# Three fused stages on one core: the RMS norm's group sum, mean and reciprocal root go from TensorE, ScalarE and VectorE to GpSimd

## The chip, the core and the metric

One core of a Trainium2 chip. A core has five engines with a queue each, in order: TensorE (PE), VectorE (DVE), ScalarE (ACT), GpSimd (POOL) and SyncE (SP, which only issues DMAs here). PE reads SBUF and writes PSUM, of which eight banks of 128 x 512 float32 are used: four (mm) for products on the way, four (acc) for sums. The metric is the time of one execution in device microseconds; lower is better.

## What is computed

```python
def _attn_ref(q, k, v, tau):            # N = 6016 rows, C = 256
    qn = q / (np.linalg.norm(q, axis=1, keepdims=True) + 1e-06)
    kn = k / (np.linalg.norm(k, axis=1, keepdims=True) + 1e-06)
    s = kn.transpose(0, 2, 1) @ qn / tau
    ...
    return (v @ a).astype(np.float32)   # a: softmax of s over the last axis

def _moe_ref(x, w_in, w_out):           # 256 -> 2048 -> 256
    h = np.maximum(x @ w_in, 0.0)
    return (h * h @ w_out).astype(np.float32)

def _moe2_ref(x, w_gate, w_val, w_out, rms_g):   # 256 -> 1536 -> 256
    rms = np.sqrt(np.mean(x * x, axis=-1, keepdims=True) + 1e-06)
    xn = x / rms * rms_g
    g = xn @ w_gate
    silu = g * (1.0 / (1.0 + np.exp(-g)))
    val = xn @ w_val
    return (silu * val @ w_out).astype(np.float32)
```

The output is `_moe2_ref(_moe_ref(_attn_ref(...)))`. The change touches `rms` and `xn` alone. Products are made in float32 quality from parts: each operand is split into a high and a low part, and three products (high by high, high by low, low by high) are added.

## The kernel before

The activations lie transposed: channels on the partitions (256 channels are two tiles of 128), rows of x along the free axis. The 6016 rows are twelve blocks (ten of 512, two of 448) in six pairs. The program runs through: the attention matrix (to some 55 us); the first MLP, blocks 0 to 3 one by one in units of `mlp1`, in which one hidden tile takes six matmuls up and six down; the first MLP for pairs 2 to 5 in `mlp1_pair`, which multiplies a pair as 2 x 2 blocks with seven products in place of eight, eight groups to a pair; the second MLP in `mlp2`, with the same seven products, twelve groups to a pair, most pairs in two visits.

Nothing is scheduled by a planner: the code writes out the order of every engine's queue. Work beside the products is a list of steps, `side` (norms and the operands made from the normed x) and `tokens` (the next pair's v operands, or weights). A group of `mlp1_pair` calls `aside()` at three places, after its second, its fifth and its last product, and each call takes one step from either list. In the second MLP a group has four such places, shared with `flow`, a list of weight preparation with lags.

A norm exists for each of blocks 0 to 3 (`norm_steps`) and each of pairs 2 to 5 (`pair_norm`). Its steps: s1 squares both channel tiles (ACT); s2 adds them and transposes 32 x 32 blocks (DVE); s3 sums runs of 32 on DVE, which leaves on partition 32i + t the sum over 32 channels of row t of a group, four such partial sums (i = 0 to 3) to a row, in `ns` (128 x 16, or 128 x 32 for a pair); s4 multiplies `ns` with `mean_w` on PE, which adds the four, divides by 256 and writes the mean to all four groups of partitions, after which ACT takes the root and DVE the reciprocal; s5 transposes the result back, spread over 32 (DVE); s6 multiplies x by it and by g (DVE, two instructions for a block, four for a pair).

s4 needs a bank of PSUM. In the units of `mlp1` it takes the next one in turn. In a group of the pairs it gets `b0` at a fixed place, and the step after it is taken at once:

```python
            if side and getattr(side[0], "takes_bank", False):
                side.pop(0)(b0)()
            aside()
```

`aside` takes no step from `side` as long as the first one there is an s4. ACT's root needs another table of functions than the Silu of the second MLP, so the last pair's norm loads that one again (`silu_table`). The step order of a pair is s1, s1, s2, s2b, s3, s4, s5, s6 four times, and then `pair_steps`, which make the seven operands of the normed pair, split them and store them to DRAM. L1417 and L881 are the DVE instructions that make the low part of a squared hidden tile, which the matmuls down (L110 to L112) read; L1473 and L1494 add on DVE from a bank; L1660 and L1649 are the like in the second MLP.

Of the kernel before, what the change touches and what calls it, by code (L numbers as in the profile page):

```python
# [28 lines left out]
def attn_moe_kernel(ctx: ExitStack, tc, q, k, v, tau, w_in, w_out, w_gate, w_val, w2, rms_g, out):  # L29
# [59 lines left out]
    for i in range(4):  # L89
        nc.gpsimd.tensor_tensor(out=mean_w[:, i], in0=ident[:, 0:32], in1=ident[:, 32:64], op=ALU.add)  # L90
        for j in (2, 3):
            nc.gpsimd.tensor_tensor(
                out=mean_w[:, i], in0=mean_w[:, i], in1=ident[:, 32 * j : 32 * j + 32], op=ALU.add
            )
    mw = mean_w.rearrange("p i e -> p (i e)")
    nc.gpsimd.tensor_scalar(out=mw, in0=mw, scalar1=1.0 / C, scalar2=1.0, op0=ALU.mult, op1=ALU.mult)
# [819 lines left out]

    def pair_state(p):
        if p not in xst:
            xst[p] = xp.tile([P, NC7, NB], F32, tag="xst", name="xst")
        return xst[p]  # L920

    def norm_steps(b, y):
# [26 lines left out]
        def s3():  # L949
            nc.vector.tensor_reduce(  # L950
                out=st["sm"][0], in_=st["w"][1].rearrange("p (g t) -> p g t", t=32), axis=AX.X, op=ALU.add
            )

        def s4(bank=None):
            ms = (mm() if bank is None else bank)[:, :G]
            nc.tensor.matmul(ms, mw, st["sm"][0], start=True, stop=True)

            def root():
                x, r = st["sm"]
                nc.scalar.activation(out=x, in_=ms, func=AF.Sqrt, bias=eps)  # L960
                nc.vector.reciprocal(out=r, in_=x)

            return root

        s4.takes_bank = True
# [15 lines left out]
    def pair_norm(p):  # L981
# [35 lines left out]
        def s3():  # L1017
            nc.vector.tensor_reduce(out=st["sm"][0], in_=turned(st["q"]), axis=AX.X, op=ALU.add)

        def s4(bank):  # L1020
            ms = bank[:, :G]
            nc.tensor.matmul(ms, mw, st["sm"][0], start=True, stop=True)

            def root():
                x, r = st["sm"]
                nc.scalar.activation(out=x, in_=ms, func=AF.Sqrt, bias=eps)
                if last:
                    silu_table()
                nc.vector.reciprocal(out=r, in_=x)

            return root

        s4.takes_bank = True
# [13 lines left out]
        for f in (s2, s2b, s3, s5):  # L1047
            f.only = "dve"
        return [only("act", s1(0)), only("act", s1(1)), s2, s2b, s3, s4, s5] + [
# [1105 lines left out]
```

## Time and profile before

| | |
|---|---|
| median of 3 runs | 1105.18 us (1105.12 to 1105.35) |
| the profiled execution | 1105.12 us, span of its instructions 1103.3 us |
| granted clock of PE over the span | 0.998 |
| busy: PE, DVE, ACT, POOL | 1093.5, 828.5, 788.3, 38.8 us |
| instructions on PE | 5122 matmuls with a weight load each |

The span runs from the first to the last instruction; the time of an execution also has what lies around it. Matmuls overlap in the records (each is listed with about 0.39 us, and the next starts 0.23 us later), so PE's progress is read from the distance of starts.

### The profile page before, as it was taken

What the parts mean: (1) busy time and instruction counts of PE and PEld (TensorE: products, weight loads), DVE (VectorE), ACT (ScalarE), POOL (GpSimd) and SP (SyncE); (2) the same over time, 40 slices, a digit from 0 to 9 for tenths busy, and PEclk for the clock granted to TensorE, in tenths of its full rate; (3) what the DMA queues carried; (4) which work ended last, traced back from release to release, by engine and by line L of the source; (5) the groups of instructions that cost most, each with busy time, mean ns of one, the idle gap of its engine ahead of it and who ended that gap; (6) DMA issues with size and microseconds to landing.
All of it is one profiled execution on the core that took longest, in us unless ns stands there. A gap on an engine that the chain in (4) does not pass through costs nothing.

```text
span 1103.3 us, 14660 instructions
## 1 busy us (share of the span) xinstructions
PE 1093.5 (99%) x5122; PEld 922.8 (84%) x5122; DVE 828.5 (75%) x1305; ACT 788.3 (71%) x1441; POOL 38.8 (4%) x72
## 2 busy tenths in 40 slices
PE   9999999999999999999999999999999999999997
PEld 8978888888788888889988888888888888888997
DVE  7988888778968968979858878686556666565655
ACT  8788888787777877877868777676655555655554
POOL 2021101000000000000000000000000000000000
PEclk9999999999999999999999999999999999999999
DMA  9643222231461471460385665204323232404001
GB/s 349 214 115 97 77 58 86 68 105 58 161 222 40 160 244 42 156 237 20 124 300 220 220 226 194 72 26 168 125 67 133 77 133 60 144 23 121 20 20 34
DMA packets 115819, 138.33 MB, mean 125 GB/s; under 512 B 52001, under 2 KB 73505, under 8 KB 115617
## 3 DMA queue, kind: packets, MB, share of 16 engines
q1 hardware_dynamic: 113472, 136.54, 36.8%
q10 hardware_dynamic: 2272, 0.85, 0.3%
q8 instruction: 40, 0.66, 0.2%
q14 instruction: 35, 0.28, 0.1%
HBM read 91.10 MB, written 46.27 MB: 125 GB/s over the span
## 4 chain that ended last, share of the span: by engine, by line
PE 95%; DVE 3%; ACT 1%; DMA 0%; issue 0%; DVEq 0%; ACTq 0%
PE mm L1555 31%; PE acc L111 13%; PE acc L112 13%; PE acc L110 13%; PE mm L1427 12%; PE mm L112 3%; PE mm L110 2%; PE mm L111 2%; PE mm L662 1%; PE acc L671 1%; PE acc L670 1%; PE acc L672 1%; PE mm L795 1%; DVE sh L1417 0%; DMA qraw<-in_k_dram 0%; DVE p L1414 0%
## 5 line engine op out<-in xcount | busy, mean ns | idle before, releaser
L1555 PE MATMUL mm<-p,gv 128*128 128x512 f32 (+1 forms) x1188 | 301.9, 387 | 0.0
L1555 PEld LDWEIGHTS mm<-p,gv 128*128 128x128 f32 x1188 | 221.9, 188 | 44.8 <-DVE hp L1635 1.0
L1660 DVE TENSOR_TENSOR sh<-hp,sh 128x512 fp32r<-128x512 f32 (+1 forms) x144 | 98.9, 687 | 111.2 <-ACT sh L1656 110.2
L1610 ACT COPY mm<-mm 128x512 f32<-128x512 f32 (+1 forms) x72 | 40.4, 562 | 157.6 <-PE mm L1555 153.6
L111 PE MATMUL acc<-sh,wo_h 128*128 128x512 f32 (+1 forms) x384 | 148.4, 386 | 0.4 <-DVE sh L1417 0.4
L110 PE MATMUL acc<-sh,wo_h 128*128 128x512 f32 (+1 forms) x384 | 148.3, 386 | 0.0
L112 PE MATMUL acc<-sh,wo_l 128*128 128x512 f32 (+1 forms) x384 | 148.2, 386 | 0.0
L110 PE MATMUL acc<-sh,w_h 128*128 128x512 f32 (+1 forms) x284 | 109.5, 385 | 0.0
L111 PE MATMUL acc<-sh,w_h 128*128 128x512 f32 (+1 forms) x284 | 109.5, 385 | 0.0
L112 PE MATMUL acc<-sh,w_l 128*128 128x512 f32 (+1 forms) x284 | 109.4, 385 | 0.0
L1417 DVE TENSOR_TENSOR sh<-p,sh 128x512 fp32r<-128x512 f32 (+1 forms) x127 | 85.8, 676 | 19.8 <-ACT p L1412 7.9
L1656 ACT CAST sh<-hp 128x512 fp32r<-128x512 f32 (+1 forms) x144 | 89.0, 618 | 2.8 <-DVE hp L1644 1.9
L1408 ACT ACTIVATE sh<-p 128x512 fp32r<-128x512 f32 (+1 forms) x127 | 78.6, 619 | 11.6 <-DVE p L1473 9.1
L111 PEld LDWEIGHTS acc<-sh,wo_h 128*128 128x128 f32 x384 | 72.1, 188 | 14.9 <-DVE sh L1417 0.8
L112 PEld LDWEIGHTS acc<-sh,wo_l 128*128 128x128 f32 x384 | 72.1, 188 | 13.7 <-DVE wo_l L182 0.3
L110 PEld LDWEIGHTS acc<-sh,wo_h 128*128 128x128 f32 x384 | 72.1, 188 | 13.4
L1555 PE MATMUL mm<-xs,gv 128*128 128x512 f32 (+1 forms) x324 | 82.6, 381 | 0.0
L1414 DVE TENSOR_TENSOR p<-p 128x512 f32<-128x512 f32 (+1 forms) x79 | 53.3, 675 | 31.8 <-ACT p L1465 31.6
L1644 DVE TENSOR_TENSOR hp<-mm,sg 128x512 f32<-128x512 f32 (+1 forms) x72 | 48.9, 679 | 34.1 <-PE mm L1555 33.4
L1635 DVE TENSOR_TENSOR hp<-mm,pu 128x512 f32<-128x512 f32 (+1 forms) x72 | 49.0, 680 | 28.0 <-ACT pu L1634 27.9
L1555 PEld LDWEIGHTS mm<-xs,gv 128*128 128x128 f32 x324 | 60.8, 188 | 10.2
L881 DVE TENSOR_TENSOR sh<-p,sh 128x512 fp32r<-128x512 f32 x64 | 45.7, 714 | 28.0 <-ACT sh L874 25.8
(282 smaller groups left out, 2178.0 us busy)
## 6 DMA issues: line engine op xcount, KB each, us to landing
p<-xd SPq DMA_DIRECT2D x102, 256.0 KB, 4.4
xd<-xp SPq DMA_DIRECT2D x66, 256.0 KB, 2.2
xs<-xd SPq DMA_DIRECT2D x12, 512.0 KB, 5.6
out_dram<-ot SPq DMA_DIRECT2D x40, 128.0 KB, 2.3
qraw<-in_q_dram SPq DMA_DIRECT2D x13, 384.0 KB, 7.2
qraw<-in_k_dram SPq DMA_DIRECT2D x13, 384.0 KB, 7.6
raw<-in_moe_w_out_dram SPq DMA_DIRECT2D x9, 512.0 KB, 3.6
raw<-in_moe_w_in_dram SPq DMA_DIRECT2D x8, 512.0 KB, 3.7
```

The lines of the kernel that those rows point to most:

```text
L110: nc.tensor.matmul(o, wh, xh, start=start, stop=False)
L111: nc.tensor.matmul(o, wh, xl, start=False, stop=False)
L112: nc.tensor.matmul(o, wl, xh, start=False, stop=stop)
L1408: nc.scalar.activation(out=st["h"], in_=r, func=AF.Square)
L1414: nc.vector.tensor_tensor(out=q, in0=r, in1=r, op=ALU.mult)
L1417: nc.vector.tensor_tensor(out=st["l"], in0=q, in1=f32(st["h"]), op=ALU.subtract)
L1427: nc.tensor.matmul(bank, m_part(a, w, g), x, start=start and j == 0, stop=j == 2, skip_group_check=not start)
L1555: nc.tensor.matmul(bank, c[:, hl, a, fs], x, start=start and j == 0, stop=j == 2, skip_group_check=not start)
L1635: add(out=h22, in0=bh, in1=w, op=ALU.add)
L1644: dve(out=h21, in0=bv, in1=sg1, op=ALU.mult)
L1656: nc.scalar.copy(out=parts[t][0], in_=x)
L1660: dve(out=pl, in0=x, in1=f32(ph), op=ALU.subtract)
```

## The change

The matrix `mean_w` goes; its tile now holds the constant -0.5 in its first part and room for copies in its second. Behind s3, a new function `invert` issues eight operations on POOL: copy partitions 64 to 127 down and add them, copy 32 to 63 down and add them, scale by 1/256 and add 1e-6, raise to the power -0.5, and copy the result of 32 partitions to the next 32 and then of 64 to the next 64. s4 remains as a step that issues nothing (two such steps for the last pair), so s5 follows one place later than s3's successor. It no longer asks for a bank, so it is taken at any place. The root on ACT, the reciprocal on DVE and the last pair's second load of the Silu table are gone.

```diff
@@ -86,14 +86,7 @@
     nc.gpsimd.memset(ones, 1.0)
 
     mean_w = wp.tile([P, 4, 32], F32, name="mean_w")
-    for i in range(4):
-        nc.gpsimd.tensor_tensor(out=mean_w[:, i], in0=ident[:, 0:32], in1=ident[:, 32:64], op=ALU.add)
-        for j in (2, 3):
-            nc.gpsimd.tensor_tensor(
-                out=mean_w[:, i], in0=mean_w[:, i], in1=ident[:, 32 * j : 32 * j + 32], op=ALU.add
-            )
-    mw = mean_w.rearrange("p i e -> p (i e)")
-    nc.gpsimd.tensor_scalar(out=mw, in0=mw, scalar1=1.0 / C, scalar2=1.0, op0=ALU.mult, op1=ALU.mult)
+    nc.gpsimd.memset(mean_w[:, 0], -0.5)
 
     eps, g_sb, tau_sb, rden = few[:, 0:1], few[:, 16 : 16 + KC], few[:, 32:33], few[:, 48 : 48 + KC]
     nc.gpsimd.memset(eps, 1e-6)
@@ -914,6 +907,19 @@
             nc.gpsimd.memset(x, 0.0)
         return [x[:, i, :G] for i in range(2)]
 
+    def invert(sm):
+
+        x, r = sm
+        G = x.shape[1]
+        minus_half, y, a = mean_w[:32, 0, :G], mean_w[:, 1, :G], x[:32]
+        for n in (64, 32):
+            nc.gpsimd.tensor_copy(out=y[:n], in_=x[n : 2 * n])
+            nc.gpsimd.tensor_tensor(out=x[:n], in0=x[:n], in1=y[:n], op=ALU.add)
+        nc.gpsimd.tensor_scalar(out=a, in0=a, scalar1=1.0 / C, scalar2=1e-6, op0=ALU.mult, op1=ALU.add)
+        nc.gpsimd.tensor_tensor(out=r[:32], in0=a, in1=minus_half, op=ALU.pow)
+        for n in (32, 64):
+            nc.gpsimd.tensor_copy(out=r[n : 2 * n], in_=r[:n])
+
     def pair_state(p):
         if p not in xst:
             xst[p] = xp.tile([P, NC7, NB], F32, tag="xst", name="xst")
@@ -950,19 +956,10 @@
             nc.vector.tensor_reduce(
                 out=st["sm"][0], in_=st["w"][1].rearrange("p (g t) -> p g t", t=32), axis=AX.X, op=ALU.add
             )
-
-        def s4(bank=None):
-            ms = (mm() if bank is None else bank)[:, :G]
-            nc.tensor.matmul(ms, mw, st["sm"][0], start=True, stop=True)
-
-            def root():
-                x, r = st["sm"]
-                nc.scalar.activation(out=x, in_=ms, func=AF.Sqrt, bias=eps)
-                nc.vector.reciprocal(out=r, in_=x)
-
-            return root
-
-        s4.takes_bank = True
+            invert(st["sm"])
+
+        def s4():
+            pass
 
         def s5():
             w = st["w"][0].rearrange("p (g t) -> p g t", t=32)
@@ -1016,21 +1013,10 @@
 
         def s3():
             nc.vector.tensor_reduce(out=st["sm"][0], in_=turned(st["q"]), axis=AX.X, op=ALU.add)
-
-        def s4(bank):
-            ms = bank[:, :G]
-            nc.tensor.matmul(ms, mw, st["sm"][0], start=True, stop=True)
-
-            def root():
-                x, r = st["sm"]
-                nc.scalar.activation(out=x, in_=ms, func=AF.Sqrt, bias=eps)
-                if last:
-                    silu_table()
-                nc.vector.reciprocal(out=r, in_=x)
-
-            return root
-
-        s4.takes_bank = True
+            invert(st["sm"])
+
+        def s4():
+            pass
 
         def s5():
             nc.vector.transpose(out=turned(st["w"]), in_=st["sm"][1].unsqueeze(2).to_broadcast([P, G, 32]))
@@ -1044,9 +1030,9 @@
 
             return f
 
-        for f in (s2, s2b, s3, s5):
+        for f in (s2, s2b, s3, s4, s5):
             f.only = "dve"
-        return [only("act", s1(0)), only("act", s1(1)), s2, s2b, s3, s4, s5] + [
+        return [only("act", s1(0)), only("act", s1(1)), s2, s2b, s3, *[s4] * (1 + last), s5] + [
             only("dve", s6(d, t)) for d in range(KC) for t in range(2)
         ]
```

The three pieces of the order below are of DVE at two places and of POOL. Line numbers differ: L969 of before is L966 in the changed kernel, L973 is L970, L1018 is L1015, L1036 is L1022, and from there on the changed kernel's are 14 lower (L1417 is L1403).

DVE around norm 5 (that of pair 2, in the third group of pair 3), before; `ns` is the small tile of the norm, `sh` a squared hidden tile, `xst` the pair's x, `vx` an operand of v:

```order
L1018 TENSOR_REDUCE ns<-q 128x32
L1414 TENSOR_TENSOR p_2446<-p_2444 128x512
L1417 TENSOR_TENSOR sh<-p_2446,sh 128x512
L1473 ISA p_2444<-mm,sh 128x512
L1029 RECIPROCAL ns<-ns 128x32
L1036 STREAM_TRANSPOSE p_3279<-ns 128x1024
L1417 TENSOR_TENSOR sh<-p_2446,sh 128x512
L1494 ISA p_2445<-mm,sh 128x512
L1417 TENSOR_TENSOR sh<-p_2446,sh 128x512
L1041 SCALAR_TENSOR_TENSOR xst<-xst,few,p_3279 128x512
L1299 TENSOR_TENSOR p_3323<-vx,p_3323 128x512
```

and the same place in the changed kernel:

```order
L1015 TENSOR_REDUCE ns<-q 128x32
L1400 TENSOR_TENSOR p_2442<-p_2440 128x512
L1403 TENSOR_TENSOR sh<-p_2442,sh 128x512
L1459 ISA p_2440<-mm,sh 128x512
L1403 TENSOR_TENSOR sh<-p_2442,sh 128x512
L1480 ISA p_2441<-mm,sh 128x512
L1403 TENSOR_TENSOR sh<-p_2442,sh 128x512
L1022 STREAM_TRANSPOSE p_3285<-ns 128x1024
L1285 TENSOR_TENSOR p_3329<-vx,p_3329 128x512
```

The reciprocal is gone, and the transpose (s5) has moved behind three instructions, to where the first s6 (L1041) stood.

DVE around norm 3 (of block 2, in the first two groups of pair 2), before, from the transpose of a v operand to the multiply with g:

```order
L1278 STREAM_TRANSPOSE vt<-vraw 128x512
L1414 TENSOR_TENSOR p_2446<-p_2445 128x512
L1417 TENSOR_TENSOR sh<-p_2446,sh 128x512
L1414 TENSOR_TENSOR p_2446<-p_2444 128x512
L1417 TENSOR_TENSOR sh<-p_2446,sh 128x512
L1473 ISA p_2444<-mm,sh 128x512
L961 RECIPROCAL ns<-ns 128x16
L969 STREAM_TRANSPOSE p_2406<-ns 128x512
```

and in the changed kernel:

```order
L1264 STREAM_TRANSPOSE vt<-vraw 128x512
L1400 TENSOR_TENSOR p_2442<-p_2441 128x512
L1403 TENSOR_TENSOR sh<-p_2442,sh 128x512
L966 STREAM_TRANSPOSE p_2402<-ns 128x512
L1400 TENSOR_TENSOR p_2442<-p_2440 128x512
L1403 TENSOR_TENSOR sh<-p_2442,sh 128x512
L1459 ISA p_2440<-mm,sh 128x512
L970 SCALAR_TENSOR_TENSOR xst<-xst,few,p_2402 128x512
```

The transpose moved ahead of the second squaring on DVE (L1414, now L1400), and the first s6 stands where the reciprocal was.

POOL at norm 5 in the changed kernel, where it had no row before; `mean_w` is now room for a copy or the constant:

```order
L916 COPY mean_w<-ns 64x32
L917 TENSOR_TENSOR ns<-ns,mean_w 64x32
L916 COPY mean_w<-ns 32x32
L917 TENSOR_TENSOR ns<-ns,mean_w 32x32
L918 TENSOR_SCALAR ns<-ns 32x32
L919 TENSOR_TENSOR ns<-ns,mean_w 32x32
L921 COPY ns<-ns 32x32
L921 COPY ns<-ns 64x32
```

The first waits for DVE, each of the others for the one before it on POOL.

## Rows read from the trace of the kernel before

**Rows 1.** The page's first part: engine, busy us (share of the span), instructions.

```profile
PE 1093.5 (99%) x5122; PEld 922.8 (84%) x5122; DVE 828.5 (75%) x1305; ACT 788.3 (71%) x1441; POOL 38.8 (4%) x72
```

**Rows 2.** Waits of PE: us in total, times, longest us.

```profile
PE acc L111 <- DVE sh L1417: 0.4, 1, 0.4
```

**Rows 3.** The chain that ended last, around norm 8: start us, us, what.

```profile
719.30 2.72 PE mm L1555 x12
...
734.50 2.72 PE mm L1555 x12
...
749.46 2.72 PE mm L1555 x12
```

**Rows 4.** PE's timeline behind norm 4: start, length, [idle before <-releaser].

```profile
282.88 0.39 PE L110 MATMUL acc<-sh,wo_h 128*128 128x512 f32 x1
283.63 0.50 PE L111 MATMUL acc<-sh,wo_h 128*128 128x512 f32 x1 [0.36 <-DVE sh L1417]
```

**Rows 5.** DVE's timeline from norm 3 to the stall behind norm 4.

```profile
256.56 0.69 DVE L1414 TENSOR_TENSOR p<-p 128x512 f32<-128x512 f32 x1 [1.91 <-ACT p L1465]
...
259.08 0.25 DVE L961 RECIPROCAL ns<-ns 128x16 f32<-128x16 f32 x1 [0.43 <-ACT ns L960]
259.37 0.71 DVE L969 STREAM_TRANSPOSE p<-ns 128x512 f32<-128x512 f32 x1
260.00 0.65 DVE L1299 TENSOR_TENSOR st<-vt,st 128x512 fp32r<-128x512 f32 x1
...
280.58 0.24 DVE L961 RECIPROCAL ns<-ns 128x16 f32<-128x16 f32 x1
...
282.88 0.69 DVE L1417 TENSOR_TENSOR sh<-p,sh 128x512 fp32r<-128x512 f32 x1
```

**Rows 6.** DVE's timeline at norm 5 and behind it.

```profile
349.50 1.21 DVE L1018 TENSOR_REDUCE ns<-q 128x32 f32<-128x1024 f32 x1
...
353.00 1.25 DVE L1036 STREAM_TRANSPOSE p<-ns 128x1024 f32<-128x1024 f32 x1
...
356.21 0.75 DVE L1041 SCALAR_TENSOR_TENSOR xst<-xst,few,p 128x512 f32<-128x512 f32 x1
...
364.73 0.69 DVE L1417 TENSOR_TENSOR sh<-p,sh 128x512 fp32r<-128x512 f32 x1 [0.61 <-ACT sh L1408]
```

**Rows 7.** PE's timeline: the readers of L1417's tiles behind norms 5 and 6.

```profile
365.68 0.39 PE L111 MATMUL acc<-sh,wo_h 128*128 128x512 f32 x1
...
447.60 0.39 PE L111 MATMUL acc<-sh,wo_h 128*128 128x512 f32 x1
```

**Rows 8.** DVE's timeline behind norm 6.

```profile
442.08 0.69 DVE L1414 TENSOR_TENSOR p<-p 128x512 f32<-128x512 f32 x1 [0.19 <-ACT p L1465]
...
446.53 0.69 DVE L1417 TENSOR_TENSOR sh<-p,sh 128x512 fp32r<-128x512 f32 x1 [0.56 <-ACT sh L1408]
```

**Rows 9.** POOL's timeline: small operations, and one of the costliest.

```profile
3.49 0.58 POOL L92 TENSOR_TENSOR mean_w<-mean_w,ident 128x32 f32<-128x32 f32 x2
...
4.36 1.06 POOL L92 TENSOR_TENSOR mean_w<-mean_w,ident 128x32 f32<-128x32 f32 x2
...
55.96 1.30 POOL L769 COPY few<-ws 32x1 f32<-32x1 f32 x6 [22.98 <-DVE ws L751]
...
172.95 1.19 POOL L303 TENSOR_TENSOR raw<-dg 128x256 f32<-128x256 f32 x1
```

**Rows 10.** DVE's timeline at norm 8.

```profile
724.41 1.08 DVE L1018 TENSOR_REDUCE ns<-q 128x28 f32<-128x896 f32 x1
...
729.57 0.65 DVE L1649 TENSOR_TENSOR sg<-mm,pu 128x512 f32<-128x512 f32 x1
```

**Rows 11.** The page's fifth part: a group, busy us, mean ns | idle before, releaser.

```profile
L1660 DVE TENSOR_TENSOR sh<-hp,sh 128x512 fp32r<-128x512 f32 (+1 forms) x144 | 98.9, 687 | 111.2 <-ACT sh L1656 110.2
```

**Rows 12.** DVE's timeline beside POOL's additions.

```profile
172.31 1.23 DVE L881 TENSOR_TENSOR sh<-p,sh 128x512 fp32r<-128x512 f32 x1
```

## The prediction

> **What bounds the kernel now.** I read the page first: PE is busy 1093.5 of 1103.3 us, DVE 75%, ACT 71%, POOL 4% [rows 1]. Then the waits of PE: of those after the start, the one in which a norm can have a hand is 0.4 us for L1417, DVE's low part of a squared tile [rows 2]. So a term counts only if it takes matmuls out of PE's stream, removes one of its few stalls, or makes a new one. A microsecond saved on ACT or DVE is worth nothing by itself. Norms are counted 1 to 8 here: 1 to 4 are those of blocks 0 to 3, 5 to 8 those of the pairs.
>
> **What the removed product costs.** In the chain that ended last, the twelve matmuls that open a group of the last stage start at 719.30, two groups on at 734.50, two groups on at 749.46 [rows 3]. The first stretch holds norm 8's product with mean_w, the second holds none: 15.20 against 14.96, 0.24 us. (Twelve matmuls take 2.72 us, so one is 0.227.) The other seven products are of the same form, two passes over 16 or 32 columns, between the same kind of neighbours, and PE waits at none of them. With 0.235 for the mean of what I read: 8 x 0.235 = **-1.88 us**.
>
> **The stall behind norm 4.** PE starts L110 at 282.88 and L111 only at 283.63, 0.52 us late, for DVE's L1417 [rows 4]. That L1417 ran from 282.88 to 283.57, at the end of a stretch in which DVE hardly idled. The change takes work out of this stretch: by DVE's order the transpose back (s5) of norm 3 now stands ahead of the L1414 of 256.56, where DVE idled 1.91 us, so its 0.63 us (259.37 to 260.00; its own length, 0.71, overlaps the next) goes into a gap, and so do the 0.43 us for which DVE waited for the root, and both reciprocals, 0.25 and 0.24 [rows 5]. That is 1.5 us less ahead of an L1417 that is 0.52 + 0.06 too late, and 0.47 of which PE takes by losing two products. The stall goes: **-0.52 us**. The bounds: -0.6, and 0 if POOL holds DVE up there (below).
>
> **The step that moves in the pairs.** In norms 5 to 7 s5 left the place beside the reciprocal and stands where the first multiply with g (s6) was; every later step of the pair slides by one place, its stores on SP too. The stores only have to land before the next stage reads them, many groups on: 0. On DVE the new place gets 1.25 us of work instead of 0.75 [rows 6], so what follows is 0.50 later. Behind it I follow the chain to L1417 at 364.73, which ends at 365.42 (it waited for ACT, whose queue stood behind a DVE result of this chain, so the 0.50 comes through). PE's reader starts at 365.68, 0.26 later [rows 7], and without norm 5's product it wants to start at 365.44. It can start at 365.42 + 0.50 + 0.06 (from DVE's end to PE's start as at 283.57 and 283.63) = 365.98: **+0.54 us**, so norm 5 gives more back than it gains. One pair later L1417 ends at 447.22 [rows 8] and its reader starts at 447.60 [rows 7]: by the same sum 447.78 against 447.37, at most +0.41. There DVE has a gap of 0.19 ahead of L1414 at 442.08 [rows 8] that takes part of the delay up, and if it is wider by then, all of it: 0 at least. I take **+0.2**. For norm 7 I found no L1417 with so little to spare: 0, bound +0.4.
>
> **The chain on POOL.** It replaces product, root and reciprocal by eight operations, each behind a wait for the one before it: four copies, two additions, one scale with a constant, one power. None is on PE's path unless DVE reaches s5 before it is done: s5 is in DVE's queue, and the L1417s and the readers of banks behind it wait too, then PE. A copy costs 0.217 (1.30 for six), an addition 0.29 (0.58 for two), and 0.53 (1.06 for two) in the stretch where DVE has its first work; the dearest row of a small tile on POOL is 1.19 us [rows 9]. The trace has no power. Lower end: 4 x 0.217 + 4 x 0.29 = 2.0 us, scale and power as cheap as an addition. Upper end: 8 x 1.19 = 9.5. DVE is busy nearly all the time around these norms, so I take the dearer addition for all, 8 x 0.53 = 4.2, and 0.7 more for the power (1.19 less 0.53): **4.9 us**.
>
> The windows for it: norm 5, from the end of the sum (349.50 + 1.21 = 350.71) to the place of s5, 356.21: 5.5 us [rows 6]; the next two pairs have the same order. Norm 4: eight DVE instructions stand between sum and s5 now, at some 0.65 each 5.2 us, and the 1.5 us won above are to spare. Norm 8: from 725.49 to the end of L1649, which stood at 729.57 behind the transpose and so comes about 1 us earlier: 3.7 us [rows 10]. There the chain is 1.2 us late. But s5 takes the time of the s6 that moved away, and DVE idles 111.2 us before L1660's 144 instructions, for ACT [rows 11]; I set it to 0, bound +1.2. Norms 1 and 2 have three units of twelve matmuls, 8 us, norm 3 a whole group. So POOL costs 0 in my sum.
>
> POOL can also hold DVE: a tensor_tensor of 128x512 took 1.23 us instead of 0.69 [rows 12] beside POOL's additions of 256 columns. That is 0.54 for a POOL operation of 1.2 us; for ones of a quarter of its length I take 0.1 each at most, 0.8 per norm, which in the pairs falls into the time that the transpose leaves there (1.25 us).
>
> Weighed against a rule: SBUF — State Buffer, section "Who interferes with whom", in the Trainium skill says that a Vector instruction with two SBUF inputs and a GpSimd instruction that reads SBUF exclude each other for the whole instruction, and that the second to issue waits for the first. The trace agrees in kind (0.69 to 1.23). Taken literally against a dense DVE queue the rule speaks against this change; what it would do is the second rival below, and the sum by it is that rival's 1113.5 us.
>
> ACT loses eight roots and three table loads. PE waits for none of them today and ACT idles 29%, so 0. The preparation of mean_w on POOL lies at the program's start, and its first reader is norm 1: 0.
>
> **The sum.** -1.88 - 0.52 + 0.54 + 0.2 = -1.66 us on the profiled execution's 1105.12 us (1103.3 of span), that is 1103.46; the median of the three runs is 0.06 higher: **1103.5 us**, 0.15% less. A difference under 0.2% (2.2 us) is about what a measurement of this kernel cannot tell from none. My forecast lies inside that.
>
> **Rivals.** *The moved step is free* (chance 0.23): the 0.50 us at norms 5 and 6 falls into a gap, or the chain through ACT does not pass it on. Then -1.88 - 0.52 = -2.4, 1102.8 us, just faster. For it: DVE idles a quarter of the time; against it: 0.26 and 0.38 us to spare are less than 0.50.
>
> *The chain outlasts its window* (0.22): each POOL operation meets a DVE instruction and waits it out, 8 x (0.27 + 0.69) = 7.7 us, or the power costs 3 us more than I gave it. Then s5 comes 2.2 us late at norms 5, 6 and 7, about 1.5 at norm 4 and 2 at norm 8: 10 us lost, 1113.5 us, slower. It decides from a chain of 5.9 us, at which four or five late norms eat the 1.66 us; beyond 6.4 us the kernel is slower by over 0.2%. For it: the window is only 0.6 us over my estimate, and the power was never seen. Against it: the transpose that leaves norm 5's window frees 1.25 us of it, and DVE's readers of PSUM and waits for ACT leave more.
>
> *Only the product goes* (0.15): the stall at norm 4 stays since POOL takes DVE's gain, 1104.0 us, no change.
>
> My own case has 0.40. Chances: faster 0.23, same 0.53 (0.40, and 0.13 of the third), slower 0.24 (0.22, and 0.02 of the third). The range is 1102.3 (free step, the stall at its 0.6 and 0.4 us of small stalls gone with ACT's load) to 1107.5 (a chain of 6.4 us). Less than 0.05 lies below, about 0.15 above. The likeliest case's own range is 1102.9 to 1104.3.
>
> **What would show it.** Right: no product with mean_w on PE; no wait of L111 near 283; a new short wait of PE for L1417 some 15 us behind the sum of norm 5; POOL's eight operations over 4 to 5.5 us from the end of DVE's sum; s5 with no idle time before it that POOL ended, but for norm 8. Wrong: DVE idle before the transpose, released by POOL, followed within some microseconds by PE waiting for DVE; or a power of several microseconds.

## The result, and the profile after

The changed kernel is slower: 1116.3 us (median of five runs, 1115.55 to 1118.47) against 1105.17 us (1104.89 to 1105.35), a ratio of 1.0104 [1.0093, 1.0115]. Forecast were 1103.5 us and a range up to 1107.5. The profiled execution took 1118.14 us, 1116.4 of it span.

The page of the changed kernel: busy times, and of the chain that ended last the shares by engine and by line. They answer to [rows 1].

```profile
PE 1097.0 (98%) x5106; PEld 921.4 (83%) x5106; DVE 824.9 (74%) x1297; ACT 783.4 (70%) x1429; POOL 88.5 (8%) x124
...
PE 90%; DVE 4%; POOL 3%; ACT 2%; issue 1%; DMA 0%; SPq 0%; DVEq 0%; POOLq 0%; ACTq 0%
PE mm L1541 29%; PE acc L104 12%; PE acc L105 12%; PE acc L103 12%; PE mm L1413 11%; PE mm L105 3%; PE mm L103 2%; PE mm L104 2%; POOL ns L919 2%; PE mm L788 1%; PE mm L655 1%; PE acc L664 1%; PE acc L663 1%; PE acc L665 1%; DVE sh L1403 1%
```

PE is listed as busy for longer although it lost eight products. POOL's share went from 4 to 8%, and more telling, POOL has come into the chain that ended last: 3% of the span, 2% in L919 alone, which is the power. That is the lead to follow.

The waits of PE in the changed kernel (the microseconds in total, how often, the longest), which answer to [rows 2]; L1403 is the L1417 of before, L1646 the L1660:

```profile
PE acc L104 <- DVE sh L1403: 7.8, 8, 2.5
PE acc L104 <- DVE sh L1646: 1.4, 1, 1.4
```

And the waits of DVE for POOL; L966 is the transpose back (s5) of a block's norm, L1022 that of a pair's:

```profile
DVE p L1022 <- POOL ns L921: 9.1, 3, 3.3
...
DVE w L1022 <- POOL ns L921: 3.9, 1, 3.9
...
DVE p L966 <- POOL ns L921: 1.9, 1, 1.9
```

PE's wait for the low part of a squared tile went from 0.4 to 7.8 us, and DVE stands 14.9 us before transposes, at five norms of eight, for POOL's last copy L921. The transpose takes the time of the wait from everything behind it in DVE's queue. Norm 5 shows the whole line of it, on POOL first (start, duration, line, operation, tile):

```profile
350.95 0.60 POOL L916 COPY mean_w<-ns 64x32 f32<-64x32 f32 x1 [69.95 <-DVE ns L1015]
351.63 0.75 POOL L917 TENSOR_TENSOR ns<-ns,mean_w 64x32 f32<-64x32 f32 x1
...
353.36 5.43 POOL L919 TENSOR_TENSOR ns<-ns,mean_w 32x32 f32<-32x32 f32 x1
358.85 0.47 POOL L921 COPY ns<-ns 32x32 f32<-32x32 f32 x2
```

From the first copy to the last it is 8.4 us (350.95 to 359.32), and 5.43 of them are the power. DVE at the same time:

```profile
349.67 1.22 DVE L1015 TENSOR_REDUCE ns<-q 128x32 f32<-128x1024 f32 x1
...
351.59 0.69 DVE L1403 TENSOR_TENSOR sh<-p,sh 128x512 fp32r<-128x512 f32 x1
...
355.77 0.69 DVE L1403 TENSOR_TENSOR sh<-p,sh 128x512 fp32r<-128x512 f32 x1 [0.38 <-ACT p L1398]
359.36 1.25 DVE L1022 STREAM_TRANSPOSE p<-ns 128x1024 f32<-128x1024 f32 x1 [2.89 <-POOL ns L921]
...
361.88 0.69 DVE L1403 TENSOR_TENSOR sh<-p,sh 128x512 fp32r<-128x512 f32 x1
```

DVE ended the sum at 350.89, did what stood between, and would have reached the transpose at 356.47; it starts at 359.36, 2.89 us late, and the L1403 of 361.88 is late with it. PE:

```profile
360.61 0.39 PE L103 MATMUL acc<-sh,wo_h 128*128 128x512 f32 x1
362.62 0.50 PE L104 MATMUL acc<-sh,wo_h 128*128 128x512 f32 x1 [1.62 <-DVE sh L1403]
```

L104 starts 2.01 us behind L103, where 0.23 is usual. So it goes at norms 4 to 8; DVE's wait is 1.92, 2.89, 2.89, 3.30 and 3.94 us. Norms 1 to 3 show none.

At norm 7 the wait has a second cost. PE's timeline there, and two stretches of the view by windows (length, then for each engine busy time and instructions, then the granted clock, the DMAs' share and their GB/s):

```profile
526.18 0.36 PE L103 MATMUL acc<-sh,wo_h 128*128 128x448 f32 x1
526.38 0.37 PE L104 MATMUL acc<-sh,wo_h 128*128 128x448 f32 x1
...
527.39 0.37 PE L103 MATMUL acc<-sh,wo_h 128*128 128x448 f32 x1
530.23 0.50 PE L104 MATMUL acc<-sh,wo_h 128*128 128x448 f32 x1 [2.47 <-DVE sh L1403]
530.54 0.56 PE L105 MATMUL acc<-sh,wo_l 128*128 128x448 f32 x1
...
533.89 0.40 PE L105 MATMUL acc<-sh,wo_l 128*128 128x448 f32 x1
```

```profile
530.00:534.00 4.00, 3.77 (x11) 3.36 (x12) 3.90 (x9) 0.65 (x2) 0.00 (x0) 0.57 0.00 0
534.00:538.00 4.00, 4.00 (x21) 3.64 (x20) 3.83 (x8) 2.42 (x5) 0.00 (x0) 1.00 0.00 0
```

Behind a stall of 2.64 us (L104 starts 2.84 behind L103, where 0.20 is usual) the mean granted clock was 0.57 for four microseconds, so some 3.4 of them at the lower of its two levels (1.2 of 2.4 GHz); a matmul of 448 columns then starts every 0.37 us instead of every 0.20. From 530.54 to 533.89 that is nine starts in 3.35 us instead of 1.80, 1.55 us more. The five runs spread over 3 us, and the longest, 1118.47 us, has the lowest mean clock, 0.996 against 0.998 and 0.999 of the others. So its excess may be more of the same; only the profiled execution has a trace, and the others' clock is not shown.

### The profile page after: what moved, and what is told of

Its sections match the earlier page's. It is cut to its first block, busy times and chain, and to the rows that moved or that the text cites. A ratio compares the mean times of both kernels' runs of the same rounds, so it can differ in the third digit from the quotient of the medians.

```text
span 1116.4 us, 14653 instructions
## 1 busy us (share of the span) xinstructions
PE 1097.0 (98%) x5106; PEld 921.4 (83%) x5106; DVE 824.9 (74%) x1297; ACT 783.4 (70%) x1429; POOL 88.5 (8%) x124
## 4 chain that ended last, share of the span: by engine, by line
PE 90%; DVE 4%; POOL 3%; ACT 2%; issue 1%; DMA 0%; SPq 0%; DVEq 0%; POOLq 0%; ACTq 0%
PE mm L1541 29%; PE acc L104 12%; PE acc L105 12%; PE acc L103 12%; PE mm L1413 11%; PE mm L105 3%; PE mm L103 2%; PE mm L104 2%; POOL ns L919 2%; PE mm L788 1%; PE mm L655 1%; PE acc L664 1%; PE acc L663 1%; PE acc L665 1%; DVE sh L1403 1%
## 5 line engine op out<-in xcount | busy, mean ns | idle before, releaser
L1646 DVE TENSOR_TENSOR sh<-hp,sh 128x512 fp32r<-128x512 f32 (+1 forms) x144 | 97.9, 680 | 111.1 <-ACT sh L1642 110.0
L104 PE MATMUL acc<-sh,wo_h 128*128 128x512 f32 (+1 forms) x384 | 149.4, 389 | 7.8 <-DVE sh L1403 7.8
L103 PE MATMUL acc<-sh,wo_h 128*128 128x512 f32 (+1 forms) x384 | 148.7, 387 | 0.1
L104 PE MATMUL acc<-sh,w_h 128*128 128x512 f32 (+1 forms) x284 | 109.6, 386 | 1.4 <-DVE sh L1646 1.4
L103 PE MATMUL acc<-sh,w_h 128*128 128x512 f32 (+1 forms) x284 | 109.5, 386 | 0.0
L1403 DVE TENSOR_TENSOR sh<-p,sh 128x512 fp32r<-128x512 f32 (+1 forms) x127 | 85.9, 677 | 26.1 <-ACT p L1398 15.3
L104 PEld LDWEIGHTS acc<-sh,wo_h 128*128 128x128 f32 x384 | 72.4, 188 | 24.3 <-DVE sh L1403 11.2
L103 PEld LDWEIGHTS acc<-sh,wo_h 128*128 128x128 f32 x384 | 72.4, 188 | 14.3 <-ACT sh L1394 1.0
L1400 DVE TENSOR_TENSOR p<-p 128x512 f32<-128x512 f32 (+1 forms) x79 | 52.8, 669 | 27.4 <-ACT p L1451 27.2
```

What stands on the lines that cost most here:

```text
L103: nc.tensor.matmul(o, wh, xh, start=start, stop=False)
L104: nc.tensor.matmul(o, wh, xl, start=False, stop=False)
L1400: nc.vector.tensor_tensor(out=q, in0=r, in1=r, op=ALU.mult)
L1403: nc.vector.tensor_tensor(out=st["l"], in0=q, in1=f32(st["h"]), op=ALU.subtract)
L1646: dve(out=pl, in0=x, in1=f32(ph), op=ALU.subtract)
```

## The experiments

Two theories stood against each other after this. **The power**: it costs 5.43 us where the sum had 1.2, the chain is too long for its window, and nothing else is wrong. **The rest of the change**: the eight operations with their hand-offs, the port that DVE and POOL may share, and the moved step would make the chain late or hold DVE up even with a cheap power. Ratios are against the kernel before, on the same chip.

| run | median us | ratio | DVE waits for POOL before s5, us |
|---|---|---|---|
| change | 1116.30 | 1.0104 [1.0093, 1.0115] | 14.9 |
| e1: multiplication for the power | 1103.14 | 0.9979 [0.9970, 0.9988] | 0 |
| e2: power on half of the columns | 1106.76 | 1.0012 [1.0003, 1.0021] | 4.9 |
| e3: root on ACT again | 1107.03 | 1.0014 [1.0005, 1.0023] | 0 (for ACT, before the reciprocal: 4.3) |
| e4: s5 one place later | 1107.50 | 1.0018 [1.0009, 1.0027] | 4.8 |
| e5: before, moved step alone | 1105.66 | 1.0004 [0.9995, 1.0012] | none |
| e6: before, POOL's chain beside it | 1126.19 | 1.0192 [1.0178, 1.0206] | none |
| e7: s5 two places later | 1105.92 | 1.0005 [0.9996, 1.0014] | 0 |
| e8: e4 with 64 partitions for the power | 1104.51 | 0.9994 [0.9985, 1.0003] | 1.9 |
| e9: before, 160 bytes of padding | 1126.12 | 1.0187 [1.0173, 1.0201] | none |
| e10: e6 with 192 bytes | 1127.08 | 1.0196 [1.0182, 1.0210] | none |
| e11: before without the product | 1102.61 | 0.9975 [0.9965, 0.9985] | none |
| e12: e8 without the scale | 1104.87 | 0.9998 [0.9989, 1.0007] | 1.7 |

**e1, a multiplication for the power.**

```diff
-        nc.gpsimd.tensor_tensor(out=r[:32], in0=a, in1=minus_half, op=ALU.pow)
+        nc.gpsimd.tensor_tensor(out=r[:32], in0=a, in1=minus_half, op=ALU.mult)
```

> The changed kernel with a multiplication in place of the power, same operands, same waits (so the normed x is another one). Theory, the power alone makes the chain too long: the multiplication takes 0.3 to 0.55 us as the additions do, the chains of the pairs take 3.3 to 4.2 us instead of 8.4, no transpose of norms 1 to 7 waits for POOL, at norm 8 by less than 1.2 us, PE's waits for L1403 go back to about 0.4 us, and the time is what was forecast for the whole change, 1103.5 us (1102.5 to 1104.5). Rival, the eight waits and the port that POOL and DVE share: DVE still waits 1 us or more for POOL at norms 5 to 7, and the time stays above 1108 us.

Measured 1103.14 us. POOL at norm 5, and DVE's transpose there:

```profile
348.88 0.61 POOL L916 COPY mean_w<-ns 64x32 f32<-64x32 f32 x1 [70.60 <-DVE ns L1015]
...
351.28 0.24 POOL L919 TENSOR_TENSOR ns<-ns,mean_w 32x32 f32<-32x32 f32 x1
351.59 0.47 POOL L921 COPY ns<-ns 32x32 f32<-32x32 f32 x2
```

```profile
354.31 1.24 DVE L1022 STREAM_TRANSPOSE p<-ns 128x1024 f32<-128x1024 f32 x1
```

The multiplication takes 0.24 us, the chain 3.2, and the transpose has no idle time before it. With one opcode exchanged the kernel is 13.2 us faster than the change and 2.1 us faster than before: the rest of the change comes out as forecast, and the power alone turns it round.

Both kernels have the same 5106 matmuls in the same order, so the profiled executions can be compared start by start. At the last matmul the change is 15.2 us behind e1: 0.5 at the program's start, then 1.5 at norm 4, 3.0 at norm 5, 3.0 at norm 6, 4.4 at norm 7 (1.55 of it the clock) and 2.8 at norm 8. Between the norms next to nothing is lost, so the five norms at which DVE waits for POOL hold the whole loss.

**e2, the power on half of the columns.** L920 is the power on the first half, L921 a multiplication on the second.

```diff
-        nc.gpsimd.tensor_tensor(out=r[:32], in0=a, in1=minus_half, op=ALU.pow)
+        h = G // 2
+        nc.gpsimd.tensor_tensor(out=r[:32, :h], in0=a[:, :h], in1=minus_half[:, :h], op=ALU.pow)
+        nc.gpsimd.tensor_tensor(out=r[:32, h:], in0=a[:, h:], in1=minus_half[:, h:], op=ALU.mult)
```

> The changed kernel with the power on half of the columns and a multiplication on the other half (so half of the scales are others). Theory, the power costs by its columns and what the chain has over its window passes on: the power takes 2.9 us at 16 columns, the chains of norms 5 and 6 some 6.2 us (8.4 less 2.5, and 0.3 for one more operation), DVE's waits for POOL fall from 2.9 to 0.7 us there, to about 1.3 at norm 7, 1.7 at norm 8 and 0.5 at norm 4, PE loses less than half of each, and the time is 1105.5 us (1104 to 1108). Rival, the power has a cost that does not depend on the columns, or the loss is not the overhang's: 1112 us or more.

Measured 1106.76 us, 1.3 above the forecast and inside its range. POOL's power and DVE's transpose at norm 5:

```profile
352.50 2.90 POOL L920 TENSOR_TENSOR ns<-ns,mean_w 32x16 f32<-32x16 f32 x1
```

```profile
356.25 1.25 DVE L1024 STREAM_TRANSPOSE p<-ns 128x1024 f32<-128x1024 f32 x1 [0.64 <-POOL ns L923]
```

The power costs by its columns: 2.90 us at 32 x 16, 5.43 at 32 x 32. The wait fell from 2.89 to 0.64. At norm 8 DVE still waited 1.91. The theory had PE lose less than half of each wait, and that missed: against e1 the run lost 3.6 us for 4.9 us of waits.

**e3, the root on ACT again.** POOL only sums and copies; mean, eps and root are one ACT instruction, the reciprocal is DVE's, both in the step that was empty.

```diff
-        nc.gpsimd.tensor_scalar(out=a, in0=a, scalar1=1.0 / C, scalar2=1e-6, op0=ALU.mult, op1=ALU.add)
-        nc.gpsimd.tensor_tensor(out=r[:32], in0=a, in1=minus_half, op=ALU.pow)
         for n in (32, 64):
-            nc.gpsimd.tensor_copy(out=r[n : 2 * n], in_=r[:n])
+            nc.gpsimd.tensor_copy(out=x[n : 2 * n], in_=x[:n])
+
+    def root(sm, last=False):
+        x, r = sm
+        nc.scalar.activation(out=x, in_=x, func=AF.Sqrt, scale=1.0 / C, bias=eps)
...
+        nc.vector.reciprocal(out=r, in_=x)
...
         def s4():
-            pass
+            root(st["sm"], last)
```

> The changed kernel with POOL's sum and copies alone (six operations, no scale and no power); the mean, eps and root are one instruction of ACT and the reciprocal one of DVE in the step that was empty, as in the kernel before, with the Silu table loaded again at the last norm. Theory, the sum over groups on POOL is harmless and the power is not: the six operations take 1.7 to 3 us, the root follows within 1.5 us, no wait of PE is new, and the time is 1103.5 us (1102.5 to 1105). Rival, any chain between the engines that long is too late for the place, or ACT's queue holds the root up: DVE waits for ACT or POOL before the transpose by 1 us or more at norms 5 to 7, and the time is 1107 us or more.

Measured 1107.03 us: the theory's number missed, the rival's reached. The root on ACT and the reciprocal on DVE at norm 5:

```profile
353.41 0.32 ACT L923 ACTIVATE ns<-ns,few 128x32 f32<-128x32 f32 x1 [2.37 <-POOL ns L919]
```

```profile
353.76 0.35 DVE L926 RECIPROCAL ns<-ns 128x32 f32<-128x32 f32 x1 [1.02 <-ACT ns L923]
```

POOL was done within 2.6 us, but the place of the empty step comes one place before s5's: ACT stood 2.37 us for POOL and DVE 1.02 for ACT. That ACT waits has a price of its own, largest at norm 4, where PE waits for a copy into a bank that stands behind the root in ACT's queue:

```profile
276.58 0.31 ACT L923 ACTIVATE ns<-ns,few 128x16 f32<-128x16 f32 x1 [3.41 <-POOL ns L919]
...
277.30 0.58 ACT L1455 COPY mm<-mm 128x512 f32<-128x512 f32 x1
...
277.93 0.96 PE L1421 MATMUL mm<-vr,c 128*128 128x512 f32 x3 [1.15 <-ACT mm L1455]
```

Taking the power away is not enough if the reader of POOL's result is moved forward as well: what counts is the distance from the sum to the first instruction that waits for it, and what else stands behind that instruction in its queue. How much of the 3.9 us against e1 is ACT's wait and how much DVE's, the run does not part.

**e4, the transpose one place later.** The power stays; one more empty step stands ahead of s5 at norms 4 to 8, and the first two multiplications with g share a place.

```diff
-        return [only("act", s1(0)), only("act", s1(1)), s2, s2b, s3, *[s4] * (1 + last), s5] + [
-            only("dve", s6(d, t)) for d in range(KC) for t in range(2)
-        ]
+        return [only("act", s1(0)), only("act", s1(1)), s2, s2b, s3, *[s4] * (2 + last), s5] + [
+            only("dve", lambda: [s6(0, t)() for t in range(2)] and None)
+        ] + [only("dve", s6(1, t)) for t in range(2)]
```

> The changed kernel with the transpose back one place later at norms 4 to 8 (one more empty step ahead of it; the first two multiplications with g share a place, so that all later steps stand where they stood). The power stays. Theory, only the overhang of the chain over its window costs: the window of norms 5 to 7 grows by three to four instructions of DVE, 2 to 3 us, the overhang falls from 2.9 us to between 0 and 0.9, and the time is 1104.5 us (1103 to 1108). Rival, POOL's eight operations cost by holding DVE up wherever they run, or whatever the norm delivers later is missed by PE: 1112 us or more.

Measured 1107.5 us, 3.0 above the theory's number, at the upper end of its range. POOL's end and DVE's transpose at norm 5:

```profile
357.41 0.47 POOL L921 COPY ns<-ns 32x32 f32<-32x32 f32 x2
```

```profile
354.94 0.69 DVE L1285 TENSOR_TENSOR p<-vx,p 128x512 fp32r<-128x512 f32 x1
...
356.33 0.69 DVE L1403 TENSOR_TENSOR sh<-p,sh 128x512 fp32r<-128x512 f32 x1
357.91 1.25 DVE L1022 STREAM_TRANSPOSE p<-ns 128x1024 f32<-128x1024 f32 x1 [0.89 <-POOL ns L921]
```

The chain is the same, 5.43 us of it the power; the later place has 2.0 us more of work ahead of it and the wait fell by just that, from 2.89 to 0.89. So a longer window shortens the wait as a shorter chain does. At norms 7 and 8 waits of 1.42 and 1.51 us were left, more than the theory's 0.9.

**e5, the moved step alone.** The kernel before with an empty step ahead of s5 in the pairs.

```diff
-        return [only("act", s1(0)), only("act", s1(1)), s2, s2b, s3, s4, s5] + [
+        return [only("act", s1(0)), only("act", s1(1)), s2, s2b, s3, s4, empty, s5] + [
```

> The kernel before with one empty step ahead of the transpose back in the pairs' norms, and nothing else: product, root and reciprocal stay where they were. Theory, the moved step is paid at norms 5 and 6 as the sum had it: without the product's gain in the same place, L1403's reader there comes some 0.3 to 0.55 us later at norm 5 and up to 0.4 at norm 6, and the time is 1105.7 us (1105.3 to 1106.4), against 1105.24 of before. Rival, the moved step is free: 1105.2 us, no new wait of PE near 365 and 447. Second rival, the place of the step is a large part of the loss: 1108 us or more.

Measured 1105.66 us, 0.45 more than before and near the theory's number, but the interval of its ratio includes 1, so the median alone does not tell it from the rival. The trace does. PE's one new wait is 0.3 us for L1420, the L1417 of before; its place on PE's timeline:

```profile
365.26 0.39 PE L110 MATMUL acc<-sh,wo_h 128*128 128x512 f32 x1
365.72 0.50 PE L111 MATMUL acc<-sh,wo_h 128*128 128x512 f32 x1
```

This is the reader of [rows 7] at 365.68: L111 stands 0.46 behind L110 where 0.23 is usual. Near 447 there is no new wait.

**e6, e9 and e10, POOL's chain beside the kernel before.** e6 adds the eight operations behind each sum, on a scratch tile that nothing else reads; the orders of PE, DVE and ACT stay.

```diff
+    shadow_t = wp.tile([P, 40], F32, name="beside")
...
             nc.vector.tensor_reduce(out=st["sm"][0], in_=turned(st["q"]), axis=AX.X, op=ALU.add)
+            shadow(st["sm"][0])
```

> The kernel before, with POOL's eight operations added behind each sum on a scratch tile that no other engine reads, the power among them; the orders of DVE, ACT and PE are those of before. Theory, POOL's work as such costs next to nothing: the power reads and writes 32 partitions and holds DVE up by under 0.1 us, the time is 1105.3 us (1104.9 to 1105.9). Rival, POOL and DVE hold each other up through the port they share: DVE's instructions beside the chains lengthen by 0.5 us or more a norm, PE waits for L1417 longer, 1107 us or more.

Measured 1126.19 us, and neither theory explains it. ACT's root now waits for POOL's reads of the sum (5.8 us at four norms) and DVE for the root (3.8 us instead of 1.3), but PE's only new wait behind them is 0.2 us. The loss grows from the first stage on, ahead of the first norm too, wherever PE multiplies 512 columns at a time; from 500 to 600 us, where most matmuls have 448, it does not grow. e9 is the scratch tile alone, one column of it set once; e10 is e6 with the tile 192 bytes long.

```diff
+    pad = wp.tile([P, 40], F32, name="pad")
+    nc.gpsimd.memset(pad[:, 32:33], -0.5)
```

> The kernel before with the tile of the run with POOL beside it alone: 160 bytes a partition, of which one memset writes a column at the start of the norms' code; no other operation is added, and all tiles behind it in SBUF lie 160 bytes further. Theory, the 21 us of that run came from where the operands lie: the matmuls of 512 columns start every 0.2317 us instead of 0.2267 in every stage, and the time is 1125 us (1122 to 1128). Rival, POOL's chains made it: 1105.2 us.

> The run with POOL's eight operations beside the kernel before, with its scratch tile 192 bytes long instead of 160, so that what lies behind it moves by three times 64 bytes. Theory, the move by a half of 64 made that run slow, and POOL's work as such costs next to nothing: matmuls every 0.2267 us, ACT's root waits for POOL's reads of the sum by up to 1.7 us at three norms, and the time is 1105.5 us (1104.9 to 1106.5). Rival, any move of the tiles makes PE slow, or POOL's work does: 1120 us or more. Second rival, POOL holds DVE up near the norms alone: 1107 to 1112 us.

e9 took 1126.12 us. Its PE timeline in the last stage:

```profile
850.68 1.55 PE L1558 MATMUL mm<-p,gv 128*128 128x512 f32 x6
852.07 0.39 PE L110 MATMUL acc<-sh,w_h 128*128 128x512 f32 x1
```

Six matmuls take 1.39 us, 0.232 each; the twelve of [rows 3] took 0.227 each. Over the whole traces of e9 and of before, the median distance of starts is 0.232 against 0.227 us for 512 columns, 0.202 against 0.203 for 448, and 0.120 in both for 256, with a granted clock of 0.999. 3830 matmuls of 512 columns at 0.005 us make some 19 of the 21 us. e9 differs from before by one memset and by where the tiles behind its own lie, so the place is what is left as a cause. e10 was as slow (1127.08 us), so my reason for choosing 192 bytes was wrong. Against its true reference, e9, e6 costs 0.07 us: no cost of POOL's chains with the power in them can be told here, with the reservation that both ran with this slower PE, which gives DVE and ACT more time.

**e7, the transpose two places later** in the pairs; all four multiplications with g share two places.

```diff
-        return [only("act", s1(0)), only("act", s1(1)), s2, s2b, s3, *[s4] * (1 + last), s5] + [
-            only("dve", s6(d, t)) for d in range(KC) for t in range(2)
+        return [only("act", s1(0)), only("act", s1(1)), s2, s2b, s3, *[s4] * (3 + last), s5] + [
+            only("dve", lambda d=d: [s6(d, t)() for t in range(2)] and None) for d in range(KC)
         ]
```

> The changed kernel with the transpose back two places later in the pairs (one later at norm 4, as in the run with one place); the four multiplications with g share two places, so later steps stand where they stood. Theory, the overhang alone costs: one place more gives 2 us, the run with one place had 0.9 to 1.5 us left at norms 5 to 8, so no transpose waits for POOL and the time is 1103.5 us (1102.8 to 1105, the upper end if the two crowded places cost 0.5 us a norm). Rival, what the norm delivers late is missed behind it or the crowded places cost PE as much: 1106 us or more.

Measured 1105.92 us. No transpose waits for POOL any more, but PE waits elsewhere:

```profile
371.73 0.39 PE L103 MATMUL acc<-sh,wo_h 128*128 128x512 f32 x1
372.66 0.50 PE L104 MATMUL acc<-sh,wo_h 128*128 128x512 f32 x1 [0.55 <-DVE sh L1403]
```

```profile
369.20 1.41 DVE L1027 SCALAR_TENSOR_TENSOR xst<-xst,few,p 128x512 f32<-128x512 f32 x2
...
371.91 0.69 DVE L1403 TENSOR_TENSOR sh<-p,sh 128x512 fp32r<-128x512 f32 x1
```

DVE has no gap from 367.20 to 373.80; two multiplications in one place (369.20, 1.41 us) push the L1403 of 371.91 back, and PE's L104 starts 0.70 late behind it. This is the rival's second half: a crowded place costs PE as well. In all, the run is 2.8 us behind e1 without any wait for POOL.

**e8 and e12, a shorter power.** e8 is e4 with the second addition arranged so that 64 partitions hold half of the columns each; four small operations more, the power on half as many columns. e12 leaves the scale out besides: ACT squares x / 16, and DVE's addition of the squares adds 1e-6 / 128.

```diff
+        nc.gpsimd.tensor_copy(out=z[:32], in_=x[32:64, :h])
+        nc.gpsimd.tensor_copy(out=z[32:64], in_=x[:32, h:])
+        nc.gpsimd.tensor_tensor(out=a[:32], in0=x[:32, :h], in1=z[:32], op=ALU.add)
+        nc.gpsimd.tensor_tensor(out=a[32:64], in0=x[32:64, h:], in1=z[32:64], op=ALU.add)
...
+        nc.gpsimd.tensor_tensor(out=z[:64], in0=a, in1=mean_w[:64, 0, :h], op=ALU.pow)
```

> The changed kernel with the transpose back one place later at norms 4 to 8, and with the second addition arranged so that 64 partitions hold half of the columns each: twelve operations in place of eight, and the power on half as many columns. Theory, the power costs by its columns and not by its partitions: 2.9 us at 64 x 16 instead of 5.4 at 32 x 32, four more small operations cost 1.1 us, the chain of the pairs takes 7.0 us instead of 8.4, the waits left by the run with one place (0.9, 0.95, 1.4 and 1.5 us) shrink to 0, 0, 0 to 0.1 and 0.4, and the time is 1103.7 us (1103 to 1105). Rival, the power costs by partitions too, or each further operation costs 0.5 us and more: no gain over that run, 1107 us or more.

> The run with the transpose one place later and the power on half as many columns, without the scale on POOL: ACT squares x / 16, and DVE's addition of the two squares adds 1e-6 / 128 as well, so the sum is the mean plus eps already. Theory, the chain of the pairs falls by 0.29 us, the waits of DVE for POOL from 0.4 to 0.1 us in the pairs and from 0.8 to 0.5 at norm 8, and the time is 1103.8 us (1103 to 1104.6). Rival, what that run still loses against the run without the power is the crowded place of the two multiplications and not the wait: 1104.5 us, unchanged.

e8 took 1104.51 us, e12 1104.87. The power of e8 at norm 5, and the waits that are left in it:

```profile
352.17 2.91 POOL L923 TENSOR_TENSOR mean_w<-mean_w 64x16 f32<-64x16 f32 x1
355.14 0.31 POOL L924 COPY ns<-mean_w 32x16 f32<-32x16 f32 x1
```

```profile
DVE p L1028 <- POOL ns L927: 1.1, 3, 0.4
...
DVE w L1028 <- POOL ns L927: 0.8, 1, 0.8
```

And the copy behind the power in e12:

```profile
354.88 0.62 POOL L923 COPY ns<-mean_w 32x16 f32<-32x16 f32 x1
```

64 partitions of 16 columns cost 2.91 us, as 32 partitions of 16 do (2.90 in e2). e8 came 0.8 us above its forecast, with waits of 0.37 us at norms 5 and 6 where 0 was expected, and is not distinguishable from before. e12 lies above its range, and its rival's number came nearer. In e12 the time that the scale had taken came back at once: at norm 5 the copy behind the power took 0.62 us instead of 0.31, so DVE's waits stayed at 1.7 us in all and the run says nothing on what the crowded places cost in e8. No version here that leaves nothing of the computation out is surely faster than before.

**e11, before without the product.** ACT takes the root of what the sum left.

```diff
-            ms = bank[:, :G]
-            nc.tensor.matmul(ms, mw, st["sm"][0], start=True, stop=True)
...
-                nc.scalar.activation(out=x, in_=ms, func=AF.Sqrt, bias=eps)
+                nc.scalar.activation(out=x, in_=x, func=AF.Sqrt, scale=1.0 / C, bias=eps)
```

> The kernel before without the eight products with mean_w; ACT takes the root of what the sum left on each partition (so the sum over the four groups is left out). Theory, the two first terms of the sum: 8 x 0.235 = 1.9 us less, and PE's 0.5 us behind norm 4 gone or not, since the transpose stays where it was: 1103.3 us (1102.6 to 1103.8). Rival, PE's time is not the products': 1105 us.

Measured 1102.61 us, 2.6 less, with an interval of 1.7 to 3.9. PE behind norm 4 in this kernel, and in e1:

```profile
281.58 0.40 PE L110 MATMUL acc<-sh,wo_h 128*128 128x512 f32 x1
282.30 0.51 PE L111 MATMUL acc<-sh,wo_h 128*128 128x512 f32 x1 [0.32 <-DVE sh L1413]
```

```profile
281.68 0.39 PE L103 MATMUL acc<-sh,wo_h 128*128 128x512 f32 x1
281.90 0.39 PE L104 MATMUL acc<-sh,wo_h 128*128 128x512 f32 x1
```

In e11 L111 still starts 0.49 us late; in e1 the distance is the usual 0.22. So the stall goes through what the change takes out of DVE's queue, not through the product.

## Why the prediction was wrong

**The step that failed** is the one that priced the power: "0.7 more for the power (1.19 less 0.53)", 1.2 us in all. It measured 5.43 us at 32 x 32, 4.81 at 32 x 28 and 2.9 to 3.4 at 32 x 16. With 2.91 and 5.43 for 16 and 32 columns a column costs 0.157 us, and 0.39 is left for the instruction; by this, 28 columns cost 4.8. The dearest known row stood in for an operation that no row had shown. The bound above it, 9.5 us for the chain, held the 8.4 that came, and the rival with a chain that outlasts its window came true; its chance of 0.22 was too low for a price that rested on nothing of its kind. The range did not fit the chances either: all of "slower" (0.24) lay above 1107.4 us, so 0.24 and not 0.15 lay above the range's end. Both signs that the prediction had named for being wrong are there: DVE idle before the transpose with PE waiting behind it, and a power of several microseconds.

**The other operations** were overpriced: seven at 0.53 are 3.7 us, and in the chain of norm 5 they and their hand-offs take 2.9 (8.4 less 5.43). Two of them, the copy and the addition on 64 partitions, run beside DVE and take 0.60 and 0.75; the other five take 1.1 together. The chain came out at 8.4 us instead of 4.9: 4.2 too little for the power, 0.8 too much for the rest.

**The windows** were right at three norms of five. Forecast were 5.5 us at norms 5 to 7, 5.2 at norm 4 and 3.7 at norm 8; by the transposes' waits they were 5.5 (350.95 to 356.47, and the same at norm 6), 5.2 and 3.3. Norm 7 has only 4.9 us (518.89 to 523.80): DVE's instructions there are of 448 columns and shorter. At norm 8 I set a chain that is 1.2 us late to 0 because DVE idles there. That was not borne out: against e1 PE lost 2.8 us there for a wait of 3.94 in the change, and 0.8 for 1.91 in e2. e1 has no wait at norm 8 only because its chain, with 2.6 us, is shorter than the window.

**The rival's price** of 10 us was 3 short: DVE's waits at norms 7 and 8 are 3.30 and 3.94 us instead of 2.2 and 2.0, and PE's clock fell once. In the change, what PE lost against e1 at a norm, without the clock, is 0.7 to 1.0 us for each microsecond of DVE's wait there (1.5 for 1.92 at norm 4, 3.0 for 2.89 at norms 5 and 6, 2.8 for 3.30 and for 3.94 at norms 7 and 8); in e2 it is 3.6 for 4.9. The runs with a later transpose (e4, e8, e12) do not price the wait alone: their crowded places cost too, as e7 shows.

**The product**, -1.88 us: e11 measured -2.6 with an interval that holds 1.9. Right as far as it can be told. **The stall behind norm 4**, -0.52 us: gone in e1, as the prediction had it, and back in the change (PE's L104 waits 1.15 us at 283.80) once the power makes DVE late. **The moved step**, +0.54 and +0.2 us: right in place at norm 5, where e1 has L104 start 0.70 us behind L103 (363.30 and 364.00), 0.47 more than usual, and e5, which keeps the product, 0.23 more. For the +0.2 at norm 6 neither run has a wait of PE; e5's median is 0.45 higher in all, inside its noise. **The whole sum without the power**, 1103.46 us: e1, 1103.14, with the POOL operations at 0 as the sum had them.

**POOL holding DVE**, 0.1 us an operation at most: DVE's L1403 at 351.59 and 355.77, beside the chain of norm 5, keeps its 0.69 us. It is POOL that waits: its addition at 351.63 ends at 352.38, just behind the L1403 that had started 0.04 us earlier and ends at 352.28; at norm 8 the addition on 64 partitions (28 columns) takes 0.24 us instead of 0.75. The Trainium skill, page SBUF — State Buffer, section "Who interferes with whom", has the second to issue wait, and these two rows agree. For the power they don't: the rule would keep DVE's L1403 and it apart, but the L1403 of 355.77 lies inside the power's span and takes its usual 0.69 us. (Spans on POOL are rough in the records.)

## What to carry to other kernels

An operation that no row of the trace shows is not priced by the dearest row that it does show: write down how much it may cost before the window is full, and if the window is as near as here (0.6 us over the estimate), measure that one operation before moving eight. A chain on an idle engine was free here up to the instruction that waits for it; beyond that most of each microsecond (0.7 to 1.0) went through to the engine that bounds the kernel. Making room by moving the waiting step later works by just the time of the work that gets ahead of it, but crowds the places behind it.

## What was unexpected in the hardware

The power on POOL costs 0.157 us a column, whether 32 or 64 partitions are used, and 0.39 us besides; at 32 x 32 that is 5.43 us against 0.24 for a multiplication on the same engine, 22 times as much. The Trainium skill, page GPSIMD Engine Reference, section "4.1 Engine selection", puts two-input additions, multiplications and maxima of a tile on GpSimd at about twice VectorE's time. The trace of the change agrees for two-input additions and subtractions of 128 x 256 that both engines run: L295 to L299 take 0.42 us on VectorE and 0.74 to 1.19 on GpSimd, 1.8 to 2.8 times as much. No run has the power on VectorE.

A tile of 160 or 192 bytes a partition more made the matmuls of 512 columns 2% slower (0.232 us instead of 0.227) and the kernel 21 us, twice what the change lost; those of 448 and of 256 columns kept their pace. Which operand it is, which distances are harmless, and why the smaller matmuls are spared, was not tried.

After one stall of 2.64 us PE's granted clock fell to 0.57 over the next four microseconds, 1.55 us more on top of the stall. At the other norms, where PE lost up to 1.8 us in one piece, the granted clock stayed at 1.00.
